# Four expert slots ahead of the full routing table, and another order of VectorE's work, in a fused attention and mixture-of-experts kernel

## The chip, the cores and the metric

The kernel runs on one core of a Trainium2 chip. The metric is the device time of one launch in microseconds (us). A core has TensorE (PE, its weight loads are shown as PEld), VectorE (DVE), ScalarE (ACT), GpSimd (POOL) and SyncE (SP). Each works through its own queue of instructions in order; semaphores tie the queues together. SP and POOL issue transfers, which 16 DMA engines carry out. TensorE writes to PSUM, from where ACT and DVE copy to SBUF.

## The reference

There are two stages. First comes attention over 4 batches, 8 heads, 768 positions and 64 values per head, with a mask in blocks of 32 positions: a block sees its neighbours, the first block, the last block and three sampled blocks, and blocks 0 and 23 see all. Then each of the 3072 tokens, now a row of 512 values, goes to the one of 8 experts with the largest logit.

```
scores = np.where(mask, scale * q @ k.T, -1e9)
x = softmax(scores) @ v                       # -> [3072, 512]
logits = x @ w_gate;  e = argmax(logits)
gate_w = softmax(logits)[e];  eom = sigmoid(x @ w_output_gate)[e]
out = gate_w * eom * (relu(x @ w1[e]) @ w2[e])   # w1[e] 512x1024, w2[e] 1024x512
```

## The kernel before

**Attention** runs as 104 units, two halves of the batch of 52 each: eight dense units (blocks 0 and 23) and 44 sparse ones (11 pairs of blocks, two batches `b`, two groups of heads). The emission is a software pipeline: in step m the list `run(...)` emits for each engine the parts of the units that are due. For a sparse unit m the scores (`pS`) are made a step or two ahead, the negated maximum (`dM`, line 507, DVE) and the exp (`aE`, line 512, ACT) come in step m, the transposes of P on PE (`pT`, line 451) in step m+2, where the copy from PSUM is ACT's (`aH`) for `b` = 0 and DVE's (`dL`, line 460) for `b` = 1, and P times V (`pO`, lines 525 and 532) in step m+3. The PSUM buffers of the transposes (`psT`) are two, and the transposes of the routing (`turn`, line 687) share them. `dD` (line 437) takes the row sums. Each engine gets its instructions in the order of `run`.

**Routing** goes by 24 tiles of 128 tokens (`tt`, 12 in each half of the batch) and by six groups of four (`RG`). For a tile: `turn` transposes x, `route_p` and `route_s` make the logits, `route_h` and `route_l` split x into two 16-bit parts, `store_x` writes these to `xscr` in DRAM. For a group: `route_a` and `route_c` (chains of small DVE operations, cut by `part`), `route_r` (places, on PE), and `route_d` scatters the tokens' numbers and factors by place into `table` in DRAM. `RT` holds the steps between these parts.

**The experts** work on slots of 128 tokens, eight pieces of 128 of the 1024 hidden columns each. 28 slots always run, four more stand under a condition. A weight piece (512 KB in `rbuf`; the even slots share one set of eight buffers and the odd slots the other) is split into two 16-bit parts, the high one by ACT (`w_h`, line 940) and the low one by DVE (`w_l`, line 946), then come 12 matmuls (`p_h`, line 957) and three, or two for a whole fp32 piece (`p_y`, lines 988 and 984). `load_w` fetches a piece on SP's queue as soon as the piece of the slot two before is split; its transfer happens only where the slot's expert differs from the one that the buffer holds. `load_t` (SP) reads a slot's 128 table rows, `load_x` (POOL, line 903) gathers its x rows, `x_t` transposes them by DMA (SP, line 910), six steps before use. Slots 0 and 1 (`NE = 2`) are special: they take the first 128 tokens of experts 0 and 1 among the first 16 tiles (group `GE = 3`, padded where there are fewer), so they need no full table, and their weights are fetched early (`prefetch_w`). All other slots get expert and table row from `plan`, a chain of DVE operations after the last group, and wait for the last scatter (`gate_set` on POOL, `gate_wait` on DVE). For slots 2 and 3 (`PEX`) the transposition is done on PE (line 915) with copies on ACT and DVE.

From step `FIRST` = 104 on, `PACE` says up to which expert step the experts' program is emitted in each attention step. `AHEAD` gives for the first nine pieces the steps at which their halves are split during attention (per piece: high part of the first half, low part, and the same of the second half). `PLAN` names the expert step of the plan.

Of the kernel before, what the change touches and what calls it, by code (L numbers as in the profile page):

```python
# [9 lines left out]
F32 = mybir.dt.float32  # L10
# [13 lines left out]
NT = NTOK // 128  # L24
# [15 lines left out]

GE = 3
NE = 2

# [7 lines left out]

PACE = -1, 0, 0, 2, 4, 7, 8, 9, 10, 11, 12, 13, 14, 15, 16, 17, 18

PLAN = 6, (20,)
AHEAD = ((73, 76, 77, 80), (81, 84, 85, 88), (89, 92, 93, 96), (96, 97, 97, 98), (97, 98, 98, 99), (99, 100, 100, 101),
         (100, 101, 101, 102), (101, 102, 102, 103), (103, 104, 104, 105))
FIN = ("_1_9_1_1", "_1_10_0_1", "_1_10_1_1")
T0 = 5
PH = {4: 3}
PEX = (2, 3)  # L60
XS = {2: 14}
XE = 102, 104
# [4 lines left out]
XG = 96, 98  # L67
RT = (1, 2, 3, 0, 2, 2, 1, 1), (1, 2, 3, 0, 2, 2, 1, 1), (1, 1, 2, 0, 1, 1, 0, 0), (1, 1, 2, 0, 1, 1, 0, 0)
PARTS = (5, 5, 4), (5, 5)
# [23 lines left out]
def tile_kernel(ctx, tc, q, k, v, sampled, wg, wcat, out):  # L93
# [21 lines left out]
    make_identity(nc, ident)  # L115
    ident16 = const.tile([128, 128], F16, name="ident16")
    nc.gpsimd.tensor_copy(ident16, ident)

# [52 lines left out]
    def setup_iota():  # L171
# [12 lines left out]
        for m, t, base in ((0, NE, 0), (1, NE + 2, 0)):  # L184
# [7 lines left out]
            places[:, NSURE + 2:, 1], pattern=[[1, NSLOT - NSURE - 2]], base=2 * half, channel_multiplier=0)  # L192
        nc.gpsimd.memset(places[:, NE + 1:NE + 2, 2], 1)

# [469 lines left out]
    def route_l(bp, i, tt):  # L664
        xq = xqs[tt]

        engine = nc.gpsimd if tt < NT - 2 else nc.vector
        engine.tensor_tensor(xq[:, :, 1], xt[bp, i], xq[:, :, 0], op=ALU.subtract)

# [85 lines left out]
    def route_c(g):  # L755
        x8, gs, rp = rs.pop(g)
        if g == GE:

            lack = rt.tile([1, NE], F32, name="lack")
            yield nc.vector.tensor_tensor(lack, lim, rp[0:1, 256:256 + NE], op=ALU.subtract)  # L760
            c0 = cums[g + 1][0:1, 0:NE]
            yield nc.vector.scalar_tensor_tensor(c0, lack, 0.0, c0, op0=ALU.max, op1=ALU.add)
# [131 lines left out]
    def xbuf(n):  # L894
        if not xbufs:
            xv = ring.tile([128, 4, 512], F32, tag="vt", name="xv", bufs=RG_V)
            xbufs.extend(qz + [xv[:, i] for i in range(3)])
        return xbufs[n % 6]

    def load_x(s):  # L900
        xgs[s] = (att.tile([128, 512], F32, tag="P", name=f"xg{s}", bufs=6) if s < NE else xbuf(2 * s)).bitcast(F16)
        src = xscr[0:128 * RG[GE][1]] if s < NE else xscr
        nc.gpsimd.indirect_dma_start(xgs[s], None, src, bass.IndirectOffsetOnAxis(ap=tabs[s][:, 1:2], axis=0))  # L903

    def x_t(s):
        t = att.tile([128, 512], F32, tag="P", name=f"xs{s}", bufs=6) if s < NE else xbuf(2 * s + 1)
        t = t.bitcast(F16)
        xs[s] = t.rearrange("p (h l e t) -> p h l e t", h=2, l=2, e=2)
        if s not in PEX:
            nc.sync.dma_start(t.rearrange("p (c t) -> p c t", t=128), xgs.pop(s), transpose=True)  # L910
            return
        xp = psS.tile([128, 1024], F16, tag="S", name=f"xgp{s}")
        xg = xgs.pop(s)
        for c in range(8):
            nc.tensor.transpose(xp[:, 128 * c:128 * c + 128], xg[:, 128 * c:128 * c + 128], ident16)  # L915
        nc.scalar.copy(t[:, 0:512], xp[:, 0:512])
        nc.vector.tensor_copy(t[:, 512:], xp[:, 512:])

# [13 lines left out]
    def whole(n):  # L932

        return n % 8 == 3 and n > 8 * NE

# [82 lines left out]
    def at(n, f, *a):  # L1018
        hooks.setdefault(n, []).append((f, a))
# [49 lines left out]
    for bp in range(2):  # L1069
# [21 lines left out]
        for n, i in enumerate(tiles):  # L1091
            tt = 12 * bp + n

            t0 = LATE.get(tt, o + 7 + 4 * n + LAGS[2] + (T0 if tt < NT - 3 else 5))
            r0, rl, r1, r2, t2, t3, t4, t5 = RT[max(0, tt + 4 - NT)]
            at(t0 + r2, turn, bp, i, tt)
# [5 lines left out]
            for g, (a, e) in enumerate(RG):  # L1102
                if e == tt + 1:

                    pa, pc = ((14,), (10,)) if e == NT else PARTS
                    t4 = t0 + t3 + len(pa) - (len(pa) > 1) + t4
                    t5 = t4 + t5
                    for m, n_ in enumerate(pa):
                        at(t0 + t3 + m, part, route_a, n_, g)
                    at(t4, route_r, g)  # L1110
                    at(t4, route_b, g)
                    for m, n_ in enumerate(pc):
                        at(t5 + m, part, route_c, n_, g)
                    t5 += len(pc) - t0 - 1
# [4 lines left out]
                    if g == GE:  # L1119
                        for s in range(NE):  # L1120
                            at(XG[0], load_t, s)
                            at(XG[1], load_x, s)

# [32 lines left out]
    def program(n0, n1, ahead=0):  # L1156
# [13 lines left out]
        for s in range(NSLOT):  # L1170
            t = 8 * s
            if s >= NE:
# [3 lines left out]
                do(max(t - 14, end + 1), 1, load_x, s, n1 + ahead)  # L1176
            do(XS.get(s, t - 6), 15, x_t, s)
            do(t + 8 + YL, 12, y_o, s)
            do(t + 8 + YL + 1, 13, store_y, s)
        for n in range(NP):  # L1180
            do(n - LEAD, 6, w_h, n)
            do(n - LEAD, 7, w_l, n)
            if n >= 8 * NE:

                free = n - 16 + YL + 1 if whole(n - 16) else n - 16 - LEAD + 1
                do(max(free, end), 1 if n < 8 * NE + 4 else 14, piece_load, n, n1 + ahead)
            do(PH.get(n, n), 8, p_h, n)
# [12 lines left out]
    for i, hl in enumerate(AHEAD):  # L1200
# [4 lines left out]
        done.update(((w_h, i), (w_l, i)))  # L1205
    for s in range(NE):
        at(XE[s], x_t, s)
        done.add((x_t, s))
    main = program(0, NSURE, 2)
    for step in range(max(max(hooks), n + 2) + 1):  # L1210
# [83 lines left out]
```

## Time and profile before

| | |
|---|---|
| median of 3 runs | 612.17 us (608.45 to 614.04) |
| the profiled execution | 611.67 us, its span 609.9 us |
| busy share of PE, DVE, ACT, POOL | 91%, 79%, 71%, 43% |
| mean granted TensorE clock | 0.960 |
| moved by DMA | 126.95 MB, mean 208 GB/s |

Times in the profile count from the first instruction of the span. A row of the order of time has start, duration, engine, line, operation, tile written and tiles read, count, and in brackets the idle time of the engine before it with what ended it. Rows of the same kind that follow each other are merged. A row of the table of stretches has the stretch and its length, the busy time of PE, PEld, DVE, ACT and POOL with the number of instructions, the granted TensorE clock, the mean busy share of the DMA engines and GB/s. A row of the waits has the engine and line that waited, what it waited for, the sum in us, the number of times and the longest. SPq and POOLq are the issuing queues.

### The profile page before, as it was taken

How to read it: one execution, taken by the hardware profiler on the slowest of the kernel's cores; microseconds unless marked ns; L12 is line 12 of the kernel's file. 1: busy time of each engine (PE TensorE's matmuls, PEld its weight loads, DVE VectorE, ACT ScalarE, POOL GpSimd, SP SyncE). 2: the span in 40 equal slices, each digit the busy share in tenths (PEclk: the TensorE clock that was granted, in tenths of full speed). 3: DMA queues.
4: the chain of work that ended last, by engine and by line, in shares of the span. 5: the costliest groups of instructions: out<-in, count | busy, mean ns of one | idle time of the engine just before them, and what ended most of it. 6: DMA issues, size and time to landing. Idle time of an engine off the chain costs nothing. (4 is left out here: it accounts for less than half of the span.)

```text
span 609.9 us, 22111 instructions
## 1 busy us (share of the span) xinstructions
PE 556.7 (91%) x8259; PEld 388.2 (64%) x8259; DVE 483.7 (79%) x934; ACT 433.7 (71%) x834; POOL 261.0 (43%) x324
## 2 busy tenths in 40 slices
PE   6879988979889879977879998999999999999996
PEld 4556656646557556646757776776777777777773
DVE  5868777758676778787768998898998989989891
ACT  2556757756567857875649887888878888888881
POOL 4395767845667847754242311312213122131311
PEclk8998989989899998986989999999999999999999
DMA  8996999975977965774183499279934925824491
GB/s 300 384 298 226 337 320 308 267 224 131 290 210 231 292 210 140 216 245 107 36 278 108 114 348 296 63 185 264 296 91 120 309 70 162 261 73 74 97 305 41
DMA packets 73724, 126.95 MB, mean 208 GB/s; under 512 B 38283, under 2 KB 44555, under 8 KB 73612
## 3 DMA queue, kind: packets, MB, share of 16 engines
q1 hardware_dynamic: 61868, 87.84, 49.4%
q0 software_dynamic: 11744, 37.64, 19.9%
q8 instruction: 67, 1.10, 0.8%
q14 instruction: 45, 0.37, 0.2%
HBM read 183.09 MB, written 20.49 MB: 334 GB/s over the span
## 5 line engine op out<-in xcount | busy, mean ns | idle before, releaser
L946 DVE SCALAR_TENSOR_TENSOR kr<-r,kr 128x1024 f16<-128x1024 f32 (+1 forms) x173 | 184.0, 1106 | 16.8 <-ACT kr L940 15.2
L940 ACT ACTIVATE kr<-r 128x1024 f16<-128x1024 f32 (+1 forms) x173 | 156.2, 958 | 1.3 <-DMA r<-in_wcat_dram 0.7
L957 PEld LDWEIGHTS <-kr 128*128 128x128 f16 x2004 | 126.0, 98 | 47.0 <-issue 9.4
L997 POOL DMA_INDIRECT out_dram<-yo,tab x28 | 29.6, 1059 | 216.8 <-ACT yo L994 202.7
L988 PE MATMUL y<-kr,hh 128*128 128x512 f16 x423 | 114.4, 380 | 0.4 <-DVE hh L975 0.4
L512 ACT ACTIVATE P<-S,mx 128x256 f32<-128x256 f32 x176 | 74.6, 481 | 35.1 <-DVE mx L507 32.6
L957 PE MATMUL h<-xv,kr 128*128 128x128 f16 x1344 | 93.3, 219 | 2.4 <-DMA xv<-qz 2.0
L946 DVE SCALAR_TENSOR_TENSOR ws<-r,ws 128x1024 f16<-128x1024 f32 (+1 forms) x60 | 71.4, 1227 | 9.0 <-ACT ws L940 8.5
L451 PE MATMUL T<-ident,P 128*128 128x128 f32 x352 | 60.2, 296 | 8.5 <-DVE den L550 6.3
L988 PEld LDWEIGHTS <-hh 128*128 128x128 f16 x594 | 50.2, 98 | 25.9 <-DVE hh L975 1.1
L507 DVE TENSOR_REDUCE mx<-S 128x2 f32<-128x512 f32 x88 | 59.5, 676 | 0.0
L500 PE MATMUL S<-kr,qz 64*32 64x256 f32 x1408 | 56.0, 410 | 3.8 <-DVE pt1d L460 2.4
L940 ACT ACTIVATE ws<-r 128x1024 f16<-128x1024 f32 (+1 forms) x60 | 57.9, 1011 | 0.8 <-PE y L988 0.8
L957 PEld LDWEIGHTS <-ws 128*128 128x128 f16 x684 | 43.9, 100 | 15.7 <-issue 5.1
L525 PEld LDWEIGHTS O<-vc,pt 128*64 128x64 f32 x704 | 29.4, 143 | 37.2 <-issue 17.4
L968 ACT ACTIVATE hh<-h 128x512 f16<-128x512 f32 (+1 forms) x56 | 30.3, 542 | 31.6 <-PE h L957 31.6
L413 POOL DMA_INDIRECT vt<-vscr,vidx x44 | 45.6, 1037 | 10.0 <-issue 7.7
L525 PE MATMUL O<-vc,pt 128*64 128x65 f32 x704 | 42.0, 241 | 8.4 <-issue 4.0
L451 PEld LDWEIGHTS T<-ident,P 128*128 128x128 f32 x352 | 39.6, 147 | 15.5 <-issue 8.9
L532 PE MATMUL O<-vt,pt 128*32 128x65 f32 x1408 | 40.8, 234 | 6.0 <-issue 3.3
L988 PE MATMUL y<-ws,hh 128*128 128x512 f16 x171 | 46.0, 379 | 0.0
L395 POOL TENSOR_TENSOR kr<-kn,eighth 128x256 f32<-128x256 f32 x66 | 40.4, 623 | 6.7 <-issue 3.1
(227 smaller groups left out, 903.4 us busy)
## 6 DMA issues: line engine op xcount, KB each, us to landing
r<-in_wcat_dram SPq DMA_DIRECT2D x240, 512.0 KB
vscr<-vn SPq DMA_DIRECT2D x12, 520.0 KB
qz<-in_q_dram SPq DMA_DIRECT2D x24, 256.0 KB
xscr<-xq SPq DMA_DIRECT2D x48, 128.0 KB
vc<-vscr SPq DMA_DIRECT2D x22, 260.0 KB
kn<-in_k_dram SPq DMA_DIRECT2D x8, 384.0 KB
vs<-in_v_dram SPq DMA_DIRECT2D x6, 512.0 KB
kn<-in_k_dram SPq DMA_DIRECT2D x6, 512.0 KB
```

What stands on the lines that cost most here:

```text
L395: nc.gpsimd.tensor_tensor(r[:, :, slot], kn[bp][:, :, ds(rv, 1)].rearrange("p u o n -> p u (o n)"), eighth.unsqueeze(2).to_broadcast([128, ...
L413: nc.gpsimd.indirect_dma_start(t[:, s].rearrange("p b j w -> p (b j w)"), None, vscr[bp], bass.IndirectOffsetOnAxis(ap=vidx[:, i, s:s + 1] ...
L451: nc.tensor.transpose(pt[:, 128 * c:128 * c + 128], p[:, 128 * c:128 * c + 128], ident)
L500: nc.tensor.matmul(u.s[64 * h2 + 32 * qi:64 * h2 + 32 * qi + 32, hp], t[p, 64 * j + 32 * qi:64 * j + 32 * qi + 32], g[p, 2 * hg + hp, 1 - ...
L507: nc.vector.tensor_reduce(mx, self.s, axis=AX.X, op=ALU.max, negate=True)
L512: nc.scalar.activation(p[:, 256 * hp:256 * hp + 256], self.s[:, hp], AF.Exp, bias=self.mx[:, hp:hp + 1])
L525: nc.tensor.matmul(o[64 * h2:64 * h2 + 64, hp, 0:VW], w[:, col:col + 64], cv[:, b, 4 * h2 + 2 * hg + hp], start=hp == 0, stop=False)
L532: nc.tensor.matmul(o[64 * h2 + 32 * qi:64 * h2 + 32 * qi + 32, hp, 0:VW], w[:, col:col + 32], av[:, qi, b, 4 * h2 + 2 * hg + hp], start=Fa ...
L940: nc.scalar.activation(w[:, 0, r], piece(n // 8, n % 8)[:, r], AF.Copy, scale=SW)
L946: nc.vector.scalar_tensor_tensor(w[:, 1, r], piece(n // 8, n % 8)[:, r], SW, w[:, 0, r], op0=ALU.mult, op1=ALU.subtract)
L957: nc.tensor.matmul(hps[n // 4][:, 128 * j:128 * j + 128], w[:, hl, 128 * c:128 * c + 128], x[:, c // 2, xl, c % 2], start=cnt == 0, stop=c ...
L988: nc.tensor.matmul(ys[s], a[:, m], w[:, l, 512:1024], start=n % 8 == 0 and cnt == 0, stop=n % 8 == 7 and cnt == 2)
```

## The change

Slots 0 to 3 now stand ahead of the full table: slots 0 and 1 as before, slots 2 and 3 with the first 128 tokens of experts 2 and 3 among the first 20 tiles (group 4). Their weights are fetched without condition, the first five pieces of slot 2 during attention (`WP2`). The PE transposition of slots 2 and 3 and its 16-bit identity are gone; all slots use the DMA. The plan moves from expert step 6 to 8, the pace of the experts' program becomes one step per attention step, the routing of the last two tiles gets the same distances as that of the others, with `route_l` on POOL throughout, and groups 0 to 2 get their routing parts four steps apart. `AHEAD` has from piece 3 on the high parts in odd and the low parts in even steps. In `run`, `dL` stands before `dM`.

```diff
-GE = 3
-NE = 2
+GE = {3: (0, 2), 4: (2, 4)}
+NE = 4
...
-PACE = -1, 0, 0, 2, 4, 7, 8, 9, 10, 11, 12, 13, 14, 15, 16, 17, 18
-
-PLAN = 6, (20,)
-AHEAD = ((73, 76, 77, 80), (81, 84, 85, 88), (89, 92, 93, 96), (96, 97, 97, 98), (97, 98, 98, 99), (99, 100, 100, 101),
-         (100, 101, 101, 102), (101, 102, 102, 103), (103, 104, 104, 105))
+PACE = -1, 0, 1, 2, 3, 4, 5, 6, 7, 8, 9, 10, 11, 12, 13, 14, 15
+
+PLAN = 8, (20,)
+AHEAD = ((73, 76, 77, 80), (81, 84, 85, 88), (89, 92, 93, 94)) + tuple((m, m + 1, m, m + 1) for m in range(95, 106, 2))
...
-PEX = (2, 3)
-XS = {2: 14}
 XE = 102, 104
...
-RT = (1, 2, 3, 0, 2, 2, 1, 1), (1, 2, 3, 0, 2, 2, 1, 1), (1, 1, 2, 0, 1, 1, 0, 0), (1, 1, 2, 0, 1, 1, 0, 0)
+
+XG2 = 2, 3
+WP2 = 97, 99, 101, 103, 105
+RT = 1, 2, 3, 0, 2, 2, 1, 1
...
-    ident16 = const.tile([128, 128], F16, name="ident16")
-    nc.gpsimd.tensor_copy(ident16, ident)
...
-        nc.gpsimd.memset(places[:, NE + 1:NE + 2, 2], 1)
+        nc.gpsimd.memset(places[:, NE:NE + 1, 2], NE - 2)
+        nc.gpsimd.memset(places[:, NE + 1:NE + 2, 2], NE - 1)
...
-        engine = nc.gpsimd if tt < NT - 2 else nc.vector
-        engine.tensor_tensor(xq[:, :, 1], xt[bp, i], xq[:, :, 0], op=ALU.subtract)
+        nc.gpsimd.tensor_tensor(xq[:, :, 1], xt[bp, i], xq[:, :, 0], op=ALU.subtract)
...
-        if g == GE:
-            nc.tensor.matmul(rp[:, 256:256 + NE], ones, cums[g + 1][:, 0:NE], start=True, stop=True)
+        if g in GE:
+            a, e = GE[g]
+            nc.tensor.matmul(rp[:, 256 + a:256 + e], ones, cums[g + 1][:, a:e], start=True, stop=True)
...
     def load_w(s, j):
+        if s < NE:
+            nc.sync.dma_start(piece(s, j), wcat[j, s])
+            return
...
-            xbufs.extend(qz + [xv[:, i] for i in range(3)])
+
+            xbufs.extend([xv[:, 2], xv[:, 3], qz[0], qz[1], xv[:, 0], xv[:, 1]])
...
-        src = xscr[0:128 * RG[GE][1]] if s < NE else xscr
+        src = xscr[0:128 * tiles_of[s]] if s < NE else xscr
...
-        if s not in PEX:
-            nc.sync.dma_start(t.rearrange("p (c t) -> p c t", t=128), xgs.pop(s), transpose=True)
-            return
-        xp = psS.tile([128, 1024], F16, tag="S", name=f"xgp{s}")
-        xg = xgs.pop(s)
-        for c in range(8):
-            nc.tensor.transpose(xp[:, 128 * c:128 * c + 128], xg[:, 128 * c:128 * c + 128], ident16)
-        nc.scalar.copy(t[:, 0:512], xp[:, 0:512])
-        nc.vector.tensor_copy(t[:, 512:], xp[:, 512:])
+        nc.sync.dma_start(t.rearrange("p (c t) -> p c t", t=128), xgs.pop(s), transpose=True)
...
+                    a0, da = t0 + t3, 1
+                    if g < 3:
+
+                        a0, da, t4, t5 = t0 + 5, 4, t0 + 14, t0 + 17
...
-    for j in range(12, 8 * NE):
+    for j in range(12, 16):
         at(2 * per - 5 + j - 12, prefetch_w, j)
+    for s in range(2):
+        at(XG[0], load_t, s)
+        at(XG[1], load_x, s)
+    for j, s in enumerate(WP2):
+        at(s, load_w, 2, j)
...
-            do(XS.get(s, t - 6), 15, x_t, s)
+            elif s > 1:
+                do(XG2[0], 2, load_t, s)
+                do(XG2[1], 1, load_x, s)
+            if s > 1:
+                do(t - 6, 15, x_t, s)
...
-        run("aE0", "dL0", "dM", "dL", "pO", "aO", "aE", "dD", "fin")
+        run("aE0", "dL0", "dL", "dM", "pO", "aO", "aE", "dD", "fin")
```

More of the change, by code (lines that the diff above doesn't have):

```diff
@@ L756, in route_c @@
         x8, gs, rp = rs.pop(g)
[L757 to L761, printed above, removed]
+        if g in GE:
+            a, e = GE[g]
+            lack = rt.tile([1, e - a], F32, tag="lack", name=f"lack{g}")
+            yield nc.vector.tensor_tensor(lack, lim[:, a:e], rp[0:1, 256 + a:256 + e], op=ALU.subtract)
+            c0 = cums[g + 1][0:1, a:e]
             yield nc.vector.scalar_tensor_tensor(c0, lack, 0.0, c0, op0=ALU.max, op1=ALU.add)
@@ L896, in xbuf @@
             xv = ring.tile([128, 4, 512], F32, tag="vt", name="xv", bufs=RG_V)
-            xbufs.extend(qz + [xv[:, i] for i in range(3)])
+            xbufs.extend([xv[:, 2], xv[:, 3], qz[0], qz[1], xv[:, 0], xv[:, 1]])
         return xbufs[n % 6]
+    tiles_of = {s: RG[g][1] for g, (a, e) in GE.items() for s in range(a, e)}
     def load_x(s):
-        xgs[s] = (att.tile([128, 512], F32, tag="P", name=f"xg{s}", bufs=6) if s < NE else xbuf(2 * s)).bitcast(F16)
-        src = xscr[0:128 * RG[GE][1]] if s < NE else xscr
+        xgs[s] = (att.tile([128, 512], F32, tag="P", name=f"xg{s}", bufs=6) if s < 2 else xbuf(2 * s)).bitcast(F16)
+        src = xscr[0:128 * tiles_of[s]] if s < NE else xscr
         nc.gpsimd.indirect_dma_start(xgs[s], None, src, bass.IndirectOffsetOnAxis(ap=tabs[s][:, 1:2], axis=0))
     def x_t(s):
-        t = att.tile([128, 512], F32, tag="P", name=f"xs{s}", bufs=6) if s < NE else xbuf(2 * s + 1)
+        t = att.tile([128, 512], F32, tag="P", name=f"xs{s}", bufs=6) if s < 2 else xbuf(2 * s + 1)
         t = t.bitcast(F16)
         xs[s] = t.rearrange("p (h l e t) -> p h l e t", h=2, l=2, e=2)
-        if s not in PEX:
-            nc.sync.dma_start(t.rearrange("p (c t) -> p c t", t=128), xgs.pop(s), transpose=True)
-            return
-        xp = psS.tile([128, 1024], F16, tag="S", name=f"xgp{s}")
-        xg = xgs.pop(s)
-        for c in range(8):
-            nc.tensor.transpose(xp[:, 128 * c:128 * c + 128], xg[:, 128 * c:128 * c + 128], ident16)
-        nc.scalar.copy(t[:, 0:512], xp[:, 0:512])
-        nc.vector.tensor_copy(t[:, 512:], xp[:, 512:])
+        nc.sync.dma_start(t.rearrange("p (c t) -> p c t", t=128), xgs.pop(s), transpose=True)
     wbuf = []
@@ L932, in whole @@
     def whole(n):
-        return n % 8 == 3 and n > 8 * NE
+        return n % 8 == 3 and n > 16
     def w_h(n, r=slice(0, 1024)):
@@ L1094, in tile_kernel @@
             t0 = LATE.get(tt, o + 7 + 4 * n + LAGS[2] + (T0 if tt < NT - 3 else 5))
-            r0, rl, r1, r2, t2, t3, t4, t5 = RT[max(0, tt + 4 - NT)]
+            r0, rl, r1, r2, t2, t3, t4, t5 = RT
             at(t0 + r2, turn, bp, i, tt)
@@ L1107, in tile_kernel @@
                     t5 = t4 + t5
+                    a0, da = t0 + t3, 1
+                    if g < 3:
+                        a0, da, t4, t5 = t0 + 5, 4, t0 + 14, t0 + 17
                     for m, n_ in enumerate(pa):
-                        at(t0 + t3 + m, part, route_a, n_, g)
+                        at(a0 + da * m, part, route_a, n_, g)
                     at(t4, route_r, g)
@@ L1112, in tile_kernel @@
                     for m, n_ in enumerate(pc):
-                        at(t5 + m, part, route_c, n_, g)
-                    t5 += len(pc) - t0 - 1
+                        at(t5 + da * m, part, route_c, n_, g)
+                    t5 += da * (len(pc) - 1) - t0
                     for t in range(a, e):
@@ L1118, in tile_kernel @@
                         at(t0 + t5 + 1, gate_set)
[L1119 to L1122, printed above, removed]
     for bp in range(2):
@@ L1182, in program @@
             do(n - LEAD, 7, w_l, n)
-            if n >= 8 * NE:
+            if n >= 16 + len(WP2):
                 free = n - 16 + YL + 1 if whole(n - 16) else n - 16 - LEAD + 1
-                do(max(free, end), 1 if n < 8 * NE + 4 else 14, piece_load, n, n1 + ahead)
+                do(max(free, end) if n >= 8 * NE else free, 1 if n < 8 * NE + 4 else 14, piece_load, n, n1 + ahead)
             do(PH.get(n, n), 8, p_h, n)
@@ L1205, in tile_kernel @@
         done.update(((w_h, i), (w_l, i)))
-    for s in range(NE):
+    for s in range(2):
         at(XE[s], x_t, s)
```

## The prediction

> **What bounds the kernel now.** I read the page's table of engines first, then the chain of work that ended last, then PE's order of time around the place where attention gives way to the experts, and last the table of short stretches for the DMA share.
>
> ```profile
> PE 556.7 (91%) x8259; PEld 388.2 (64%) x8259; DVE 483.7 (79%) x934; ACT 433.7 (71%) x834; POOL 261.0 (43%) x324
> 530.00:575.00 45.00, 45.00 (x503) 32.45 (x501) 40.89 (x43) 37.63 (x51) 10.46 (x8) 1.00 0.35 74
> ```
>
> TensorE is busy for 91% of the span, and in 530 to 575 us for all of it. In the expert part the time is therefore TensorE's work plus its gaps. A step is one eighth of a slot; I write T(k) for the start of PE's first matmul of piece k, so slot s begins at T(8s).
>
> ```profile
> 307.54 0.81 PE L988 MATMUL y<-kr,hh 128*128 128x512 f16 x3
> 312.92 1.03 PE L915 MATMUL xgp<-ident,xv 128*128 128x128 f16 x8 [4.56 <-DMA xv<-xscr,tab]
> 313.74 1.49 PE L957 MATMUL h<-xs,kr 128*128 128x128 f16 x12
> 316.10 0.83 PE L957 MATMUL h<-xv,kr 128*128 128x128 f16 x12
> ...
> 320.05 0.61 PE L915 MATMUL xgp<-ident,qz 128*128 128x128 f16 x8
> ...
> 327.08 0.83 PE L957 MATMUL h<-qz,ws 128*128 128x128 f16 x12
> ...
> 337.89 0.83 PE L957 MATMUL h<-xv,kr 128*128 128x128 f16 x12
> ...
> 359.50 0.83 PE L957 MATMUL h<-qz,ws 128*128 128x128 f16 x12
> ...
> 372.49 0.83 PE L957 MATMUL h<-xv,kr 128*128 128x128 f16 x12 [2.02 <-DMA xv<-qz]
> ```
>
> These are the starts of slots 2, 3, 4, 6 and 7 (the operand `xv` or `qz` changes with the slot): 316.10, 327.08, 337.89, 359.50 and 372.49 us. Three slots from 327.08 to 359.50 make 10.81 us a slot. Two gaps matter: 4.56 us before 312.92, where the x rows of slot 2 are late, and 2.02 us before 372.49, where the transposed x of slot 7 is late.
>
> ```profile
> 305.15 7.72 DMA xv<-xscr,tab
> 302.63 1.50 SPq L880 DMA_DIRECT2D tab<-table  x2
> 305.15 2.88 POOL L903 DMA_INDIRECT xv<-xscr,tab  x1 [6.70 <-DMA r<-in_wcat_dram]
> 363.86 3.88 SPq L910 DMA_TRANSPOSE xv<-qz  x1
> ```
>
> The chain starts with the first line: the gather needs its table rows (302.63), and these need all the tiles' scatters. So the first gap is the latency of the full table.
>
> **The change part by part.** *The table leaves the path.* Slots 2 and 3 now take experts 2 and 3 from the first 20 tiles, so 32 pieces instead of 16 stand before the table. The gap of 4.56 us, the eight transposes at 312.92 (0.82 us to the next start) and the slow matmuls after the gap go (316.10 - 313.74 = 2.36 us for a piece that takes 1.35 elsewhere: 1.0 us). What is late next is VectorE.
>
> ```profile
> 298.49 0.14 DVE L804 COPY gate<-gate 1x1 f32<-1x1 f32 x1 [1.24 <-POOL gate L801]
> 298.56 3.47 DVE L946 SCALAR_TENSOR_TENSOR kr<-r,kr 128x1024 f16<-128x1024 f32 x3
> 307.70 2.34 DVE L946 SCALAR_TENSOR_TENSOR kr<-r,kr 128x1024 f16<-128x1024 f32 x2
> 288.62 2.72 PE L957 MATMUL h<-xs,ws 128*128 128x128 f16 x24
> ```
>
> VectorE's splits of pieces 9 to 17 run without a break from 298.56 to 310.04, behind the plan and the gate; that of piece 16 ends at about 308.9. After the change two splits stand ahead of the plan (plan at step 8, split 9 at step 6), but the gate still waits for POOL's last scatter. The two subtractions for the last tiles go to POOL, and piece 8's two halves come in their place, about 1.2 us each way. So I keep split 16 near its old time and take T(16) = 309.0, between 306.6 (TensorE alone: its first expert matmul moves from 288.62 to about 287, behind the last routing transposes, and the same work follows) and 310.5 (the gate comes 1.5 us later, behind two more gathers on POOL). Against 316.10 that is **-7.1 us at slot 2**. At slot 3 the second set of transposes at 320.05 goes as well (0.45 us to the next start).
>
> *Two more experts are loaded.* Slots 2 and 3 put experts 2 and 3 over experts 0 and 1 in the weight buffers, and slot 4 needs expert 0 again. By the reference's own routing of its inputs (tiles of 128 per expert: 4, 1, 2, 1, 2, 2, 5, 11; both plans need just 28 slots, so the guarded four stay out) weights are fetched before the change for slots 3, 7, 8, 12, 14, 18, 22, after it for 2, 3, 4, 5, 7, 10, 12, 16, 20. Four adjacent slots load at the start. The prices:
>
> ```profile
> 305.00:310.00 5.00, 3.35 (x35) 2.03 (x32) 5.00 (x5) 1.97 (x3) 4.54 (x2) 1.00 0.50 152
> 310.00:315.00 5.00, 2.08 (x20) 2.09 (x21) 0.44 (x2) 1.01 (x2) 2.61 (x3) 0.75 0.96 286
> 315.00:320.00 5.00, 5.00 (x51) 3.31 (x49) 4.47 (x6) 3.42 (x5) 0.27 (x1) 0.91 1.00 393
> 320.00:325.00 5.00, 5.00 (x64) 3.89 (x63) 3.41 (x5) 4.30 (x7) 0.00 (x0) 1.00 0.57 222
> ...
> 345.00:350.00 5.00, 5.00 (x59) 3.60 (x57) 4.04 (x5) 4.26 (x7) 2.47 (x2) 1.00 0.58 145
> ...
> 550.00:555.00 5.00, 5.00 (x61) 3.70 (x59) 4.92 (x5) 3.28 (x6) 0.00 (x0) 1.00 0.40 56
> ```
>
> The last two columns are the busy share of the 16 DMA engines and GB/s. Without weights a slot costs 0.35 x 10.81 = 3.8 us of DMA; a stretch of few bytes and much share (550 to 555) is a transpose, 0.40 x 5 = 2.0 us, which leaves 0.9 each for gather and store. Slot 3's eight pieces with three gathers and a store took (0.50+0.96+1.00+0.57) x 5 = 15.2 us, so a piece takes (15.2 - 3.6)/8 = 1.45 us. Slot 7's stall gives a second value: DMA gets busy at about 347.1 (0.58 of 345 to 350), the transposed x lands at 372.3, and in these 25.2 us lie 12 pieces, two transposes, two gathers, a store: (25.2 - 6.7)/12 = 1.54 with nothing fixed, 1.40 with 1.7 us of latency. I take 1.40 and 1.7.
>
> Transposes are issued on SP's queue behind the weights (363.86, 8.4 us to landing), six steps ahead of use. After the change the pieces of slot 2 from the sixth on, and all of slots 3 and 4, queue in one run from about 291.5 us, when SP is through with the last x stores. Before the transpose of slot 4 stand 23 pieces, four gathers (slots 2 to 5), two transposes, two stores: 23 x 1.40 + 3.6 + 3 x 2.0 (its own with them) + 1.8 + 1.7 = 45.3 us, so slot 4 starts at 336.8, not at 309.0 + 21.6 = 330.6: new stalls of 6.2 us, some 2 at slot 3 and 4 at slot 4. At slot 5 only four more pieces are queued and the backlog is gone. Against 337.89 there is **-1.1 us** left at slot 4. A piece at 1.54 us puts 3.2 on top; 1.30 takes 2.3 off.
>
> By the Trainium skill (DMA: Bandwidth & Descriptors, Specifications) HBM gives a core about 358 GB/s; a piece of 524,288 bytes would then be an estimated 1.46 us and slot 4 would start 1.4 us later than in my sum. The 393 GB/s of 315 to 320 stands above that limit. By TensorE: Matmul & The Clock Gate (Part 1) the clock halves after an idle window of about 3.4 us; the slow 1.49 us after 4.56 idle and the unchanged 0.83 after 2.02 agree; by it a stall of about 4 us at slot 4 would bring the slow clock back.
>
> The first five pieces of slot 2 are fetched during attention's last ten steps, on SP's queue between the x stores:
>
> ```profile
> 256.00:288.00 32.00, 26.18 (x455) 17.36 (x451) 26.55 (x73) 21.71 (x55) 15.88 (x16) 0.80 0.68 187
> ```
>
> 7.0 us of DMA where 0.32 x 32 = 10.2 are free: nothing, or some of the 1.5 us that attention is allowed below if the last V gathers come late.
>
> *Slot 7* loads beside no neighbour after the change, so its 2.02 us go: **-2.0 us**. Slots 10, 12, 16 and 20 load alone, as slots 12 to 22 do now without a gap of note.
>
> *Attention.* In a step VectorE copies P's transpose and then finds the maximum (0.60 us each, from start to start), not the other way round.
>
> ```profile
> 265.37 0.68 DVE L460 COPY pt<-T 128x512 f32<-128x512 f32 x1
> 266.19 0.63 PE L451 MATMUL T<-ident,P 128*128 128x128 f32 x4 [1.73 <-DVE den L550]
> 241.37 0.68 DVE L507 TENSOR_REDUCE mx<-S 128x2 f32<-128x512 f32 x1
> 241.97 0.67 DVE L460 COPY pt<-T 128x512 f32<-128x512 f32 x1
> 242.09 0.84 ACT L512 ACTIVATE P<-S,mx 128x256 f32<-128x256 f32 x2 [1.08 <-DVE mx L507]
> 243.52 0.66 PE L451 MATMUL T<-ident,P 128*128 128x128 f32 x4
> PE T L451 <- DVE den L550: 3.6, 3, 1.7
> PE O L525 <- DVE den L437: 2.4, 4, 1.3
> ACT P L512 <- DVE mx L507: 32.6, 43, 2.6
> ```
>
> At 266.19 the next transpose waited until the copy at 265.37 had emptied its PSUM buffer; 0.60 earlier helps each of the three such waits from 185 to 285 us: -1.8. On the other side P, which is done at 242.93, comes 0.60 later, against 0.59 of slack to 243.52: next to nothing, taken as +0.3 over the run. The second wait (line 525) hangs on the operation behind both, so it stays. The splits in even steps are as many and meet the steps without a copy; I count them at nothing, as the DVE work stays the same, with -2.4 (all of that wait gone) and +3 as ends. **-1.5 us**. The routing parts spread over four steps and the missing 16-bit identity lie beside a VectorE and a POOL with idle time: nothing.
>
> **The sum** on the profiled run: -1.1 - 2.0 - 1.5 = -4.6, and 611.67 - 4.6 = 607.1 us (span 609.9 and 1.8 around it). The median shown is 612.17, 0.5 above that run; I forecast **607 us**.
>
> **Rivals.** *The transposes land in time.* If they overtake the weights or DMA has more to give, no new stall comes: -7.1 - 0.45 - 2.0 - 1.5 = -11.1, so 600.6. For it speaks the 393 GB/s of one stretch; against it slot 7's stall, with less queued. *More congestion:* 1.54 us a piece, and after the longer stall a slow start like that at 313.74: 607.1 + 3.2 + 1.0 = 611.3. *Slower, through the order in attention:* where VectorE is not behind, the copy must first wait for PE's own transpose of that step (about 0.6 us), which the maximum covered. P is then about 1.2 late against 0.59 of slack, and 22 odd steps in the second half of the batch pay 0.65 us each, 14.3: 607.1 + 1.8 + 14.3 = 623.2. It decides from the point at which the wait passes the slack; against it: VectorE's idle time ahead of the copy is small where the splits run. *The table stays on the path:* the gate's wait stands in VectorE's queue ahead of splits 11 and on; if POOL's gathers for slots 2 and 3 push the gate past 302 us, T(16) is 311 to 312, but slot 4 is bound by DMA and hardly moves: the forecast again.
>
> **Chances:** forecast (603 to 609) 0.47, in-time transposes 0.23, more congestion 0.20, slower 0.10. One per cent is 6.1 us, about what this kernel's runs can tell from no change (they spread from 608.45 to 614.04). About two fifths of the forecast's band lie below 606.0, so faster by over 1% has 0.23 + 0.19 = 0.42, within 1% 0.47, slower 0.11. The range, 598 to 616, takes in the first two rivals with attention's ends, and leaves out the slow one.
>
> **What would show it.** PE without a gap from about 292 to the start of slot 3; slot 2 near 309; then gaps before the first matmul of slots 3 and 4 that end with the transposed x landing, DMA share near 1.0 from 292 to 335; no gap at slot 7. ACT's waits for the maximum grow above the 32.6 us of the row. I am wrong if the gaps at slots 3 and 4 are missing (then faster), or if attention ends more than 3 us from where it does now.

## The result and the profile after

The change made the kernel slower: 628.16 us median of 4 runs (626.9 to 631.17) against 612.97 us (608.45 to 614.04) for the kernel before beside it, a ratio of 1.028 (95% interval 1.023 to 1.033). The forecast was 607. The profiled execution took 626.9 us, its span 625.0. Here and below, ratios leave out the slower executions and medians take in all, and the two can differ, because the kernel before scatters widely (598.8 to 617.6 us in one set). First the page's row for the engines and the one for the DMA bytes:

```profile
PE 558.6 (89%) x8244; PEld 387.8 (62%) x8244; DVE 487.1 (78%) x932; ACT 432.1 (69%) x832; POOL 263.2 (42%) x326
DMA packets 78139, 135.86 MB, mean 217 GB/s; under 512 B 40651, under 2 KB 46923, under 8 KB 78028
```

TensorE has the same work (558.6 us against 556.7) in a span that is 15.1 us longer. The DMA engines carry 8.91 MB more: 16 weight pieces of two more experts (8.39 MB) and the two transpositions that TensorE made before (0.52 MB). PE's order of time, with the end of attention, the first gap among the experts, and the first matmul of slots 2, 3, 4, 6 and 7:

```profile
298.07 0.66 PE L531 MATMUL O<-vt,pt 128*32 128x65 f32 x16
...
317.01 0.61 PE L985 MATMUL y<-kr,hh 128*128 128x512 f16 x1 [3.10 <-DVE hh L972]
317.42 1.49 PE L954 MATMUL h<-xs,kr 128*128 128x128 f16 x12
...
328.64 0.83 PE L954 MATMUL h<-xv,kr 128*128 128x128 f16 x12 [3.17 <-DMA xv<-xv]
...
341.29 0.83 PE L954 MATMUL h<-xv,ws 128*128 128x128 f16 x12 [1.95 <-ACT kr L937]
...
355.03 0.83 PE L954 MATMUL h<-qz,kr 128*128 128x128 f16 x12 [2.77 <-DMA qz<-qz]
...
376.64 0.83 PE L954 MATMUL h<-xv,ws 128*128 128x128 f16 x12
...
387.45 0.83 PE L954 MATMUL h<-qz,kr 128*128 128x128 f16 x12
```

Attention's last P·V (line 531) ends at 298.73 us; before it ended at 284.71. These 14.0 us are nearly the whole loss. From there to the end of the span it is 326.3 us, before 325.2: the four slots gave nothing and cost about one. The forecast had named an end of attention more than 3 us from the old one as a sign of being wrong, and this sign came. The waits, after first and then before:

```profile
ACT P L511 <- DVE mx L506: 57.1, 63, 3.2
DVE den L436 <- ACT ob L540: 24.7, 22, 6.8
PE O L524 <- DVE den L436: 12.3, 12, 4.1
ACT ob L540 <- POOL x L440: 5.8, 2, 5.3
```
```profile
DVE den L437 <- ACT ob L541: 14.0, 20, 4.9
PE O L525 <- DVE den L437: 2.7, 5, 1.3
```

ACT waits 57.1 us for the maximum where it waited 32.6; TensorE waits for the row sums (`den`) 12.3 us where it waited 2.7. The loss is in attention, in the loop of VectorE, ACT and TensorE. Two edits touch it, the order of the step and the spread routing parts, and the forecast had counted both as small.

### The profile page after: what moved, and what is told of

Read it like the earlier page. It is cut to its first block, busy times and chain, and to the rows that moved or that the text cites. A ratio compares the mean times of both kernels' runs of the same rounds, so it can differ in the third digit from the quotient of the medians.

```text
span 625.0 us, 22006 instructions
## 1 busy us (share of the span) xinstructions
PE 558.6 (89%) x8244; PEld 387.8 (62%) x8244; DVE 487.1 (78%) x932; ACT 432.1 (69%) x832; POOL 263.2 (42%) x326
## 4 chain that ended last, share of the span: by engine, by line
issue 23%; DMA 14%; PE 10%; POOL 3%; DVE 1%; ACT 1%; SPq 1%; POOLq 0%; ACTq 0%; DVEq 0%
DMA out_dram<-yo,tab 9%; PE h L954 5%; PE y L985 4%; DMA xv<-xv 2%; DMA qz<-qz 1%; DMA table<-vals,place 1%; POOL xv L908 1%; PE y L981 1%; DVE kr L943 1%; ACT kr L937 1%; POOL out_dram L994 1%; POOL table L789 1%; POOL qz L908 0%; SPq L891 0%; DVE ws L943 0%
## 5 line engine op out<-in xcount | busy, mean ns | idle before, releaser
L943 DVE SCALAR_TENSOR_TENSOR kr<-r,kr 128x1024 f16<-128x1024 f32 (+1 forms) x173 | 186.5, 1122 | 21.1 <-ACT kr L937 20.3
L511 ACT ACTIVATE P<-S,mx 128x256 f32<-128x256 f32 x176 | 74.2, 475 | 62.0 <-DVE mx L506 57.1
L954 PE MATMUL h<-xv,kr 128*128 128x128 f16 x1404 | 97.5, 219 | 3.2 <-DMA xv<-xv 3.2
L943 DVE SCALAR_TENSOR_TENSOR ws<-r,ws 128x1024 f16<-128x1024 f32 (+1 forms) x60 | 69.9, 1202 | 10.0 <-ACT ws L937 9.4
L499 PE MATMUL S<-kr,qz 64*32 64x256 f32 x1408 | 57.9, 406 | 6.8 <-ACT kr L392 2.5
L524 PE MATMUL O<-vc,pt 128*64 128x65 f32 x704 | 41.7, 240 | 12.6 <-DVE den L436 12.3
L687 DVE TENSOR_TENSOR xT<-xp,xT 128x512 f16<-128x512 f32 x24 | 16.6, 692 | 36.9 <-ACT xT L686 36.9
```

The lines of the kernel that those rows point to most:

```text
L499: nc.tensor.matmul(u.s[64 * h2 + 32 * qi:64 * h2 + 32 * qi + 32, hp], t[p, 64 * j + 32 * qi:64 * j + 32 * qi + 32], g[p, 2 * hg + hp, 1 - ...
L511: nc.scalar.activation(p[:, 256 * hp:256 * hp + 256], self.s[:, hp], AF.Exp, bias=self.mx[:, hp:hp + 1])
L524: nc.tensor.matmul(o[64 * h2:64 * h2 + 64, hp, 0:VW], w[:, col:col + 64], cv[:, b, 4 * h2 + 2 * hg + hp], start=hp == 0, stop=False)
L943: nc.vector.scalar_tensor_tensor(w[:, 1, r], piece(n // 8, n % 8)[:, r], SW, w[:, 0, r], op0=ALU.mult, op1=ALU.subtract)
L954: nc.tensor.matmul(hps[n // 4][:, 128 * j:128 * j + 128], w[:, hl, 128 * c:128 * c + 128], x[:, c // 2, xl, c % 2], start=cnt == 0, stop=c ...
```

## The experiments

The kernels ran on several chips, always beside runs of before, whose medians were 609.3 to 613.0 us there (620.7 on one slower chip). I go by each kernel's distance from the median of before beside it, and give the ratio with its 95% interval. A profile is one execution: four kernels whose attention is the same (the four slots alone and the three versions with early x) ended it at 281.3 to 289.2 us, so a single end of attention is good to some 4 us each way.

### Attention: the order of the step, and the spread parts

Two edits, each undone in the changed kernel, as the lines show, and each made alone in the kernel before:

```diff
-        run("aE0", "dL0", "dL", "dM", "pO", "aO", "aE", "dD", "fin")
+        run("aE0", "dL0", "dM", "dL", "pO", "aO", "aE", "dD", "fin")    # old order
```
```diff
-                    if g < 3:
+                    if g < 0:                                            # parts one step apart
```

The changed kernel with the old order:

> The changed kernel with the old order in a step (maximum, then copy). Order theory: VectorE's later maximum holds ScalarE's queue, so of the 14.0 us by which attention ends later (298.7 against 284.7 us) at least 9 go; last P times V ends at 285 to 290 us, time 613 to 619 us. Rival, the splits in even steps or the spread routing parts: attention still ends after 296 us, time 625 to 629 us.

The kernel before with the new order:

> The kernel before with only the new order in a step (copy, then maximum). Order theory: 9 to 14 us slower than before, 621 to 627 us, ScalarE's wait for the maximum above 45 us in all instead of 32.6. Rival (the order does little by itself): 610 to 616 us.

The changed kernel with the old places of the splits (`AHEAD`), which lays no blame on either:

> The changed kernel with the old steps of the first nine pieces' splits. Order theory: the splits matter only in the last ten steps, attention ends at 295 to 299 us, time 624 to 629 us. Rival, the even steps: attention ends before 290 us, 614 to 619 us.

The spread undone, with the new order and with the old one:

> The changed kernel with the routing parts of the first three groups one step apart again, as before; VectorE's order in a step stays the new one. Theory: of the 14.0 us by which attention's last P.V came later, most comes from the spread parts (GpSimd's scatter waits for VectorE's place numbers while the finish of an output block stands behind it), so the last P.V comes at 288 to 292 us and the time is 617 to 622 us. Rival, the spread harmless and the order alone at fault: the last P.V stays at 297 us or later and the time at 625 us or above.

> The changed kernel with the old order in a step and the routing parts of the first three groups one step apart: what is left is the four slots without the full table, their pieces, the transpositions and the splits in even steps. Theory: attention's last P.V comes at 284 to 288 us and the expert part lasts as long behind it as in the changed kernel (326 us), so 609 to 615 us: the same as before. Rival, that the four slots themselves hold attention up: last P.V at 290 us or later, time 617 us or above. My forecast's own account of the four slots, if attention is as before: 605 to 609 us.

The spread alone and both edits together, in the kernel before:

> The kernel before with the routing parts of the first three groups four steps apart, nothing else. Theory: a delay of 5 to 8 us in VectorE's maxima between the 48th and the 54th unit that stays to the end, last P.V at 289 to 292 us, time 616 to 620 us. Rival, the spread harmful only beside the other edits: last P.V within 2 us of before's 284.7 and time 610 to 614 us.

> The kernel before with both edits of attention, the new order in a step and the parts of the first three groups four steps apart, but three slots and the full table as they were. If the two add up, last P.V at 291 to 294 us and time 619 to 623 us (order alone gave 5.1 us on the medians, spread alone 6.2); if they cost more together, or only beside the four slots, 625 us or more, or 615 us or less.

Measured, as the median, its distance from the median of before beside it, and the end of attention in the profile:

| | three slots (before) | four slots |
|---|---|---|
| neither | 609 to 613, 284.7 | 613.0, +3.6, 284.9 |
| new order | 614.5, +3.5, 287.3 | 619.6, +10.3, 292.7 |
| spread parts | 615.6, +6.3, 289.5 | 618.9, +7.9, 292.2 |
| both | 623.7, +14.5, 297.0 | 628.2, +15.2, 298.7 |

Ratios, left column downwards: 1.019 (1.014 to 1.024), 1.014 (1.009 to 1.019), 1.023 (1.015 to 1.031); right: 1.006 (1.002 to 1.011), 1.017 (1.009 to 1.025), 1.011 (1.003 to 1.020) and after's 1.028. The splits' old places gave 625.7 us (1.021) and an end of attention at 300.4: not the cause. The two edits make 14.5 us in the kernel before without any fourth slot, and without them the changed kernel is within 1.1% of before: the loss is theirs. The old order alone brought the time into the band of its theory (613 to 619), but attention's end into neither band, so the order was not all of it. The four slots alone (with the change's steps for the splits and for the last tiles) end at +3.6 by the medians: not the 3 us of gain that my sum gives without attention's 1.5. The new order alone gave 614.5 us, not the 621 to 627 that I expected after the first look; its ratio would make it 11 us rather than 3.5, its end of attention, 2.6 us later, speaks for the smaller figure. Alone the edits make 3.5 and 6.3 us in the kernel before, so 4.7 of the 14.5 would come only when both are there, and the sum expected (619 to 623) was just passed. But beside the four slots the single edits (6.7 and 4.3) make 11.0 of 11.6, and by the ratios 1.9% and 1.4% stand against 2.3%. That the two make each other larger is not shown.

Why the order costs is in one step of the two traces, the same step in both. Before, the maximum at 241.37, the copy at 241.97 and the exp at 242.09 stand in the prediction; the rest of the step, first before, then the kernel before with the new order:

```profile
244.11 0.28 ACT L541 COPY ob<-O 128x130 f32<-128x130 f32 x1
244.42 0.16 DVE L437 TENSOR_SCALAR den<-O 128x2 f32<-128x2 f32 x1 [0.32 <-ACT ob L541]
244.50 0.68 DVE L507 TENSOR_REDUCE mx<-S 128x2 f32<-128x512 f32 x1
```
```profile
242.10 0.68 DVE L460 COPY pt<-T 128x512 f32<-128x512 f32 x1
242.71 0.67 DVE L507 TENSOR_REDUCE mx<-S 128x2 f32<-128x512 f32 x1
243.41 0.84 ACT L512 ACTIVATE P<-S,mx 128x256 f32<-128x256 f32 x2 [1.67 <-DVE mx L507]
245.44 0.29 ACT L541 COPY ob<-O 128x130 f32<-128x130 f32 x1
245.75 0.16 DVE L437 TENSOR_SCALAR den<-O 128x2 f32<-128x2 f32 x1 [0.92 <-ACT ob L541]
245.83 0.68 DVE L460 COPY pt<-T 128x512 f32<-128x512 f32 x1
```

The loop goes maximum on VectorE, exp on ACT, behind it on ACT the copy of O (`ob`), which the row sums on VectorE wait for, and behind these the next maximum. Before, VectorE's copy of the transposed P lay beside ACT's exp and cost nothing: from the first VectorE operation at 241.37 to the row after `den` at 244.50 are 3.13 us. With the copy ahead of the maximum it stands inside the loop: 242.10 to 245.83 are 3.73 us, 0.60 more, the whole copy. ACT's exp has waited 1.67 us instead of 1.08, and VectorE 0.92 for `ob` instead of 0.32. So the loop binds in such steps, and TensorE, whose slack to P I had measured, comes second. Part of the loss is taken back on the way: of VectorE's 88 maxima of the sparse units, the 36th comes 6.3 us later with the new order (124.42 against 118.09), the last one 2.7 us later (279.88 against 277.15).

### Why the spread parts cost

In the changed kernel with the old order, GpSimd's scatter waits for the spread parts, and the finish of an output block (`x`) stands behind it:

```profile
183.02 1.04 POOL L789 DMA_INDIRECT table<-vals,place  x1 [4.47 <-DVE rnm L711]
...
187.11 0.62 POOL L440 TENSOR_TENSOR x<-ob0d,den0d 128x256 f32<-128x256 f32 x1
187.76 0.27 ACT L540 COPY ob<-O 128x130 f32<-128x130 f32 x1 [5.30 <-POOL x L440]
188.06 0.16 DVE L436 TENSOR_SCALAR den<-O 128x2 f32<-128x2 f32 x1 [3.39 <-ACT ob L540]
188.28 0.70 PE L524 MATMUL O<-vc,pt 128*64 128x65 f32 x8 [3.71 <-DVE den L436]
```

It looked like the cause: a stop of 5.3 us that runs from GpSimd through ACT and VectorE to TensorE, once in each kernel with spread parts at these steps. To take it away, the scatters of the first three groups were called three steps later (`t0 + t5 + 4` in place of `+ 1` at `route_d`):

> The changed kernel with the old order in a step and the parts still four steps apart, but the scatters of the first three groups (route_d) called three steps later, so that the place numbers are ready when GpSimd comes to them. Theory, the scatter's wait in GpSimd's order is how the spread parts hold attention up: no jump between the 48th and the 54th maximum against the kernel before (within 2 us, where the old order with spread parts had 8), last P.V at 284 to 287 us, time 611 to 614 us. Rival, the spread parts cost on VectorE or TensorE themselves: last P.V stays at 290 to 293 us and the time at 617 to 620 us.

The stop went (ACT's wait of 5.30 us fell to 0.91), the time did not: 617.8 us, +8.6 (1.014, 1.007 to 1.021), attention's end at 291.0. My theory fell. The next two runs spread two groups only (`if g < 2`), and left the parts together with the scatters 14 steps later:

> The changed kernel with the old order and only the first two groups' parts four steps apart; the third group's, which fall into the first units of the second pair of batches, one step apart. Theory, the third group's parts cost most because they stand among the second pass's first units: the maxima after the 50th unit come within 4 us of the four slots alone, last P.V at 285 to 288 us, time 613 to 615 us. Rival, each group costs alike (about 2 us): last P.V at 289 to 290 us, time 616 to 618 us.

> The four slots alone (old order, all parts one step apart) with only the scatters of the first three groups 14 steps later, about where the spread parts put them. If the lateness of the scatters in GpSimd's order is what costs, last P.V at 289 to 292 us and 617 to 620 us, as with spread parts; if VectorE's spread parts cost (their small instructions held while GpSimd works, 6.4 us over their usual length with spread parts against 2.9 us without), last P.V stays at 284 to 287 us and the time at 611 to 614 us.

Two groups: 617.7 us, +7.7 (1.012, 1.005 to 1.019), attention's end at 289.1, so the third group is not the dear one. Late scatters alone: 611.3 us, +1.3 (0.999, 0.994 to 1.004), end at 284.4: they cost nothing. What is left are VectorE's parts themselves. One thing that they meet is seen in the run with spread parts and scatters three steps later, VectorE first, then GpSimd:

```profile
184.32 2.11 DVE L775 SCALAR_TENSOR_TENSOR se<-se,gs 128x4 f32<-128x4 f32 x1
```
```profile
184.65 0.62 POOL L440 TENSOR_TENSOR x<-ob0d,den0d 128x256 f32<-128x256 f32 x1
185.22 0.62 POOL L440 TENSOR_TENSOR x<-ob1d,den1d 128x256 f32<-128x256 f32 x1
185.79 0.61 POOL L394 TENSOR_TENSOR kr<-kn,eighth 128x256 f32<-128x256 f32 x1
```

An operation on 128x4 numbers that takes 0.15 us elsewhere lasts until GpSimd's third row in a run is over (186.40). The Trainium skill (SBUF — State Buffer, Who interferes with whom) says that a VectorE instruction with two inputs in SBUF and a GpSimd instruction that reads SBUF exclude each other; this row agrees. Over all parts such holds, counted as the excess over an operation's usual length, add up to some 6.4 us with the spread parts and 2.9 without. To see whether they decide, the spread parts were moved as a whole by one, two and three steps (`t0 + 5`, `t0 + 14` and `t0 + 17` each plus 1, 2 or 3), which changes what GpSimd does beside them and keeps the spacing:

> The changed kernel with the old order and the spread routing parts (4 steps apart as there) all one step later, so that they fall on another of the four steps in which a tile's work repeats, and GpSimd does other work beside them. Theory, the parts cost because VectorE's small instructions are held while GpSimd works: their excess over the usual length (6.4 us unshifted, 2.9 us unspread) changes, and time moves with it: at an excess near 3 us, 612 to 615 us; at 6 us or more, 617 us or more. Rival, the spacing itself costs (five steps of every kind, further behind): 617 to 620 us whatever the excess.

> The same, two steps later. Theory and rival as for one step: the time follows the excess of the parts (612 to 615 us at 3 us, 617 us or more at 6 us), or stays at 617 to 620 us.

> The same, three steps later: the time follows the excess of the parts (612 to 615 us at 3 us, 617 us or more at 6 us), or stays at 617 to 620 us.

These three ran on the slower chip (before 620.7 us), some 10 us above the figures expected: 628.4, 624.9 and 620.0 us, distances of +7.7, +4.2 and -0.7 us (1.013, 1.007 to 1.019; 1.006, 1.003 to 1.010; 0.999, 0.996 to 1.002), where the unshifted parts had +7.9. On one chip and with one spacing, then, two steps of shift change the time by 8.4 us: it is not the spacing alone that costs. Nor do the holds decide: they came to some 4.9, 2.2 and 4.2 us in these runs. What decides is where the parts fall; whether that is the step among a tile's four or their place beside the dense units no run tells, as none moves them by four. A reservation: the unshifted parts and the four slots alone were not run on that chip. The expert part lasts 324.5 to 325.3 us in these three, as elsewhere, so what makes the chip slower shows in attention, and the -0.7 hangs on before being slower there too.

Where the parts cost can be seen from the same 88 maxima, of which every kernel makes as many. The 44th and the 51st, with the old order and spread parts unshifted, then shifted by three steps:

```profile
133.88 0.68 DVE L506 TENSOR_REDUCE mx<-S 128x2 f32<-128x512 f32 x1
...
189.82 0.68 DVE L506 TENSOR_REDUCE mx<-S 128x2 f32<-128x512 f32 x1
```
```profile
138.84 0.68 DVE L506 TENSOR_REDUCE mx<-S 128x2 f32<-128x512 f32 x1
...
185.62 0.68 DVE L506 TENSOR_REDUCE mx<-S 128x2 f32<-128x512 f32 x1
```

This stretch, in which the dense units of the second half lie, takes 55.94 and 46.78 us. In all eight kernels with spread parts at the old steps it takes 50.6 to 55.9 us, with a shift of one step 52.4, of two 46.3, and in the eight kernels with the parts together 43.2 to 46.3 (before 44.26). So most of what the parts cost arises here and not evenly over their steps, and the shifts by two and three take most of it away. VectorE is busy for 37.3 of the 55.9 us, and for 35.0 of 43.2 in the four slots alone: the parts bring some 2 us of work and over 12 of time, so most of it is waiting. The whole costs less than this stretch, as the spread parts let attention come to the 44th maximum earlier (133.88 against 141.20). Coming early is not itself the reason for the longer stretch: the kernel with slot 2's x early, its parts together, was there at 135.34 and took 44.99 us. Which wait starts the loss, no run shows.

### The four slots: what their x waits for

In the changed kernel SyncE's queue, GpSimd's last scatter and the gate read:

```profile
306.90 9.82 SPq L887 DMA_DIRECT2D r<-in_wcat_dram  x7
321.83 0.36 SPq L879 DMA_DIRECT2D tab<-table  x1
322.75 1.29 SPq L914 DMA_TRANSPOSE xv<-xv  x1
```
```profile
313.96 0.97 POOL L789 DMA_INDIRECT table<-vals,place  x1 [0.30 <-issue]
315.05 0.14 DVE L803 COPY gate<-gate 1x1 f32<-1x1 f32 x1 [1.72 <-POOL gate L800]
```

The chain of work that ended last has the transfers between them:

```profile
313.96 7.66 DMA table<-vals,place
322.75 5.75 DMA xv<-xv
```

The row at 321.83 is slot 4's table read. It must wait until the last scatter (313.96) has landed, 7.66 us later, and slot 2's transposition, which needs no table, stands behind it: issued at 322.75, it lands 5.75 us later, and its x ends the gap at 328.64. So the full table still held slot 2, through SyncE's order. VectorE's plan and its wait at the gate (1.72 us) make a gap of their own at 317.01 (3.10 us).

Plan and gate two expert steps later (`PLAN = 10`), with the old order:

> As e1_old_order, with the plan at expert step 10 instead of 8, so that the gate's wait on VectorE and the table rows of slot 4 on SP's queue come behind the transposition of slot 2's x. Theory (the full table still stands on the path, by the queues): slot 2 starts at most 25 us after the last P times V instead of 30, and the time is 3 to 6 us under e1. Rival (the weights' DMA bounds slot 4 anyway): slot 2 starts earlier, slot 4 at the same distance, the time is that of e1 within 1.5 us.

616.9 us against 618.9 beside it (1.009, 1.005 to 1.014), 2.0 us less, between the two theories and within what the runs scatter: the gate's gap shrank to 0.95 and 0.39 us, but slot 2's transposition stood behind eight weight pieces, landed 13.48 us after its issue, and slot 2 waited 5.88 us for its x. Then, from the four slots alone, slot 2's transposition ahead of the pieces, and next all three early:

```diff
-                do(t - 6, 15, x_t, s)
+                do(4 if s == 2 else t - 6, 15, x_t, s)                  # slot 2 early; PLAN = 10
+                do({2: 4, 3: 5, 4: 21}.get(s, t - 6), 15, x_t, s)       # all early; then 4: 24
```

> The four slots alone (old order, parts one step apart) with the weight pieces of slot 2 planned later by two units and its DMA transposition put in ahead of them in SyncE's order. Theory A, SyncE's order decides: slot 2 starts within 23 us of attention's last P.V with no wait for x, and the time is 3 to 5 us under that of the four slots alone. Theory B, the transfers decide: what slot 2 gains, slots 3 and 4 wait for, slot 4 starts as far behind the last P.V as in the four slots alone (within 1 us) and so does the end: within 2 us.

> The four slots alone (old order, parts one step apart) with all three transpositions early in SyncE's order: slot 2's ahead of its weight pieces, slot 3's right behind it, slot 4's five units sooner than planned. Theory A, SyncE's order decides when x is there: slot 3 starts without a wait, slot 4 waits 4 us at most, the first matmul of slot 4 comes within 51 us of attention's last P.V (55.7 with slot 2's alone early), and the time is 604 to 607 us, below the kernel before. Theory B, the transfers decide, the 16 DMA engines being full of weights: the wait only moves to a weight piece or to slot 4's x, slot 4 starts 54 to 56 us behind the last P.V, time 609 to 613 us.

> All transpositions early as in the run before, but slot 4's three units later in SyncE's order, so that fewer weight pieces wait behind it while its gather is under way (SyncE stood still from 321.8 to 328.5 us and a weight piece came 6.5 us late). Theory, order and transfers trade against each other: slot 4 waits longer (3 to 5 us) but the 6.5 us gap behind it goes, together 3 to 4 us better: 607 to 610 us. Rival, the sum of the waits stays: 611 to 613 us.

Slot 2 early: 609.7 us, +0.3 (1.009, 1.004 to 1.015; the ratio puts it further from before than the medians do); all early: 612.3, +3.0 (1.005, 1.002 to 1.009); slot 4 later again: 612.5, +2.4 (1.004, 1.000 to 1.007). The four slots alone had +3.6, so all are within some 3 us of each other and of before. Rows of PE, one fence per kernel in this order, and for the second SyncE, ACT and GpSimd:

```profile
305.18 0.83 PE L954 MATMUL h<-xv,kr 128*128 128x128 f16 x12
...
323.23 1.44 PE L954 MATMUL h<-xv,ws 128*128 128x128 f16 x12 [7.34 <-DMA xv<-xv]
...
336.98 0.83 PE L954 MATMUL h<-qz,kr 128*128 128x128 f16 x12 [1.27 <-DMA qz<-qz]
```
```profile
332.16 0.83 PE L954 MATMUL h<-qz,kr 128*128 128x128 f16 x12 [1.19 <-DMA qz<-qz]
342.42 1.46 PE L985 MATMUL y<-kr,hh 128*128 128x512 f16 x3 [6.52 <-ACT hh L965]
...
318.54 3.25 SPq L891 DMA_DIRECT2D r<-in_wcat_dram  x4
328.49 1.29 SPq L914 DMA_TRANSPOSE qz<-qz  x1
...
341.25 0.63 ACT L937 ACTIVATE kr<-r 128x512 f16<-128x512 f32 x1 [11.24 <-DMA r<-in_wcat_dram]
...
319.38 2.96 POOL L908 DMA_INDIRECT qz<-xscr,tab  x1 [10.95 <-DMA tab<-table]
```
```profile
342.54 1.44 PE L954 MATMUL h<-qz,kr 128*128 128x128 f16 x12 [8.36 <-DMA qz<-qz]
```

With slot 2 early it starts at 305.18, 23.9 us behind attention's end (281.29) and without a wait; slot 3 then waits 7.34 us and slot 4 starts 55.7 us behind that end (54.2 in the four slots alone). With all three early, slots 2 and 3 do not wait and slot 4 starts 46.2 us behind, 8 us better, as SyncE's order would have it; but SyncE stood still from 321.8 to 328.5 us for slot 4's gather, the next weight piece came to ACT at 341.25, and TensorE lost 6.52 us. With the transposition three units later the 6.52 go and 8.36 come back at slot 4. The expert part lasts 325.6, 325.5, 324.1 and 325.1 us in these four kernels, 325.2 before. So theory A held for slot 4's start and theory B for the time: whichever transfer goes first, the sum of the waits stays. Why: two stretches of the table of stretches, after, then before:

```profile
305.00:335.00 30.00, 23.34 (x269) 16.91 (x266) 24.25 (x52) 18.69 (x26) 9.61 (x10) 0.94 0.99 281
335.00:360.00 25.00, 20.28 (x223) 14.29 (x222) 19.58 (x19) 16.73 (x22) 4.76 (x4) 1.00 1.08 347
```
```profile
305.00:335.00 30.00, 25.44 (x274) 18.43 (x272) 23.32 (x26) 20.18 (x28) 10.59 (x6) 0.94 0.59 196
335.00:360.00 25.00, 25.00 (x279) 18.04 (x278) 22.83 (x24) 20.86 (x29) 6.60 (x6) 1.00 0.64 185
```

With four experts to load at the start, the DMA engines are full for 55 us (shares of 0.99 and 1.08; the mean of a stretch can come out above 1), where before they were busy for 0.59 and 0.64. In the four slots alone and the three versions with early x the shares are 0.95 to 1.06 over the 55 us that begin 6.3 us behind attention's end. The chain scatter, table row, gather, transposition for slot 4 runs through these full engines, and weight pieces put behind it come late, as the 6.52 us show. That the bytes set the sum is the reading of these rows and of the three orders that came out alike; a run with fewer bytes was not made.

No version beats the kernel before by more than the measurement tells: the best are the spread parts shifted by three and the four slots alone with late scatters, both 0.999 of before.

## Why the prediction was wrong

- **Attention's order, "-1.5".** The step that failed first. I priced the late exp by TensorE's slack ("0.59 of slack to 243.52: next to nothing"). But the exp is part of the loop through `ob` and `den` back to VectorE, which has no such slack: 0.60 us a step where it binds, by the medians 3.5 us in the kernel before and 6.7 beside four slots. The three waits for `psT` that I hoped to save are 1.8 us against this. My slower rival had the order and a price of 14.3, but the wrong mechanism: VectorE hardly waits for TensorE's transposes of the sparse units in the new order (1.2 us in all of attention), the copy just takes its own time.
- **Spread routing parts, "nothing".** This step failed too. They cost 6.3 us alone and 4 to 5 in the four-slot kernels. "A VectorE and a POOL with idle time" was a mean over the span and says nothing of what waits for the parts: between the 44th and the 51st maximum VectorE is idle for a third of the time (old order), and that stretch still takes 5 to 13 us more with the parts spread. With the same spacing and other steps they cost nothing that can be told (-0.7, on the slower chip). Which wait makes the cost stays open.
- **Both together.** 14.5 us in the kernel before and 11.6 beside four slots, where the single edits make 9.8 and 11.0. My sum had nothing for two delays of one loop that make each other larger; whether they do is open.
- **Slot 2, "-7.1".** It started 29.9 us behind attention's end (328.64 - 298.73), before 31.4: -1.5. I named the gate's wait but let DMA cover it, and I did not walk slot 2's transposition through SyncE's queue past slot 4's table read. With it moved ahead, and the plan two steps later, slot 2 came 23.9 us behind the end, where I had said 24.3 (309.0 - 284.7).
- **Stalls at slots 3 and 4, "6.2".** Near in size: from slot 2 to slot 4 are 26.39 us where two slots take 21.6, so 4.8. The cause is the forecast one at slot 4, whose gap of 2.77 us ends with its x; the 1.95 us at slot 3 end with ACT's split of a weight piece. Slot 4 came 56.3 us behind attention's end, 54.2 with the old order and parts together, against 52.1 forecast (336.8 - 284.7).
- **Slot 7, "-2.0".** Right: slots 6 and 7 start 10.81 us apart, no gap.
- **Splits in even steps, nothing.** Right: their old places changed no time.
- **Range.** It took in no cost for the parts and +3 for the order. Had the bounds come from the copy's own 0.60 in each of its 22 steps of the second half (13 us), it would have reached about 622, and the spread would still have been missing.

## What to carry to other kernels

Before you reorder operations on an engine, follow the loop over all engines back to that engine: an operation that lies beside another engine's work is free only in that place. An engine's mean idle time says nothing of the step into which you put work; the same work, moved by two steps, changed the time by 8.4 us here. When a transfer stops depending on something, check that what stands ahead of it in its issuing queue has stopped too, and that full DMA engines do not just move the wait to the next transfer.

## What the hardware showed that I had not expected

- A VectorE operation of 0.15 us held for 2.11 us beside three GpSimd operations in a row (rows above): it ended only with the third (186.43 against 186.40).
- A table read of 2 KB issued behind weight pieces (at 309.72 in the kernel with all x early) let its gather start only at 319.38: 9.7 us, of which the transfer took 8.85.
- Half clock after a gap: the matmul groups behind 7.34 and 8.36 us of idle time took 1.44 instead of the usual 0.83. But so did the one behind 2.33 us in the run with a shift of two steps (337.56, granted clock 0.50 from 338 to 340), and the group at 317.42 behind the gap of 3.10 us took 1.49, while those behind 2.77 and 3.17 us took 0.83. The Trainium skill (TensorE: Matmul & The Clock Gate, Part 1) puts the idle window at about 3.4 us; the long gaps agree, those of 2.33 and 3.10 us do not. The length of the gap alone does not tell the clock here.
